# Gelu ahead of the probabilities, squares and sums a step sooner, a normalization behind the gate bank's reading

## The chip, the cores and the metric

The kernel runs on one core of a Trainium2 chip. What counts is the device time of one execution, in microseconds (us); a profile of one further execution shows when each engine worked. The engines are TensorE (PE, its weight loads PEld), VectorE (DVE), ScalarE (ACT), GpSimd (POOL) and SyncE (SP), which issues the transfers.

## What is computed

Two branches read the same 2048 tokens of 576 features, and a gate mixes them:

```
g = sigmoid((x * gate_w).sum(-1, keepdims=True))
a = attention with a memory(x, wq, wk, wv, wo, beta)      # 32 heads of 18, 4 segments of 512 tokens
    ...   p = softmax(q k^T * scale + mask); a_dot = p v  # inside a segment
b = (gelu(x @ w_gate) * (x @ w_up)) @ w_down              # 576 -> 4608 -> 576
out = g * a + (1 - g) * b
```

## The kernel before

Every float32 operand is split into two float16 words, high and low, and a product is made of three matmuls (high by high, high by low, low by high). After a first part of some 212 us (projections, memory), a loop of 72 steps `v` interleaves both branches; the change lies in its steps 3, 4 and 5, the fourth to sixth.

**The feed-forward branch in a step.** Step `v` takes 128 of the 4608 columns (`f = v // 2`) and two chunks of 512 tokens (`c` and `e`). Gate and up products of the two chunks are made together, in a form with seven products in place of eight; their sums grow in three PSUM banks, `V`, `G` and `U`. A step's PE work starts with the product `V` (`first_product`), then `G` from `A11`, which starts that bank anew. VectorE copies `V` to a tile `gl` (`g1`) and `G` to `U`; later `gl` plus a bank is the gate's value, ScalarE takes `gelu` of it in place, and `hidden` (L1073) multiplies it by what the bank `G` (chunk `c`) or `U` (chunk `e`) holds. Until that multiplication has read the bank, the next step's product cannot start in it. `hidden_pair` then makes the words `hh` on ScalarE and GpSimd. From step 4 on, `chains` (L1051) multiply an earlier block's `hh` by the down weights in the two banks `dn`, and VectorE adds them up (L1057).

**Attention in a step.** A unit `a` is one head in one segment; two units go through a step. `scores(a)` makes four products in banks `st` and `dn` (in the paired steps also `pv`); the pieces `put(a, i)` (L954) bring them to the tile `pf` with their row maxima. `powers` (L971, L974) takes the exponentials on ScalarE, `pair_rows` makes the words `ph` (ScalarE L984, GpSimd L985), `turn_rows` has SP issue their transposition (L991), `values` (L1005) multiplies by the values in bank `pv`, and `normalize` (L1015 to L1022) divides on VectorE. The odd unit of a head goes through `powers` and what follows in the next step.

**Weights for later steps.** `squares` sum the squares of raw weights (ScalarE L85 or VectorE L81), `sums()` turns them into scales: one small matmul into a bank `st` (L234), six short VectorE operations on it (L236 to L244) and six on GpSimd. `weights_first` scales or adds raw weights on GpSimd (L278, L299 to L303), `weights_high` and `weights_low` make their words (ScalarE L309, GpSimd L313).

The four compute engines issue in the order in which the code is written (`manual_schedule`), so where a call stands decides what waits behind it. SP's order is set by a scheduler. ScalarE holds one set of function tables: between exponentials and gelu it loads the other (`ACT_TABLE_LOAD`).

Steps 0 to 4 go through `step`, from step 5 on through `paired_step`; at the start of a step `end_pair` finishes what the former step left in `ends`.

Of the kernel before, what the change touches and what calls it, by code (L numbers as in the profile page):

```python
# [42 lines left out]
def kernel(ctx: ExitStack, tc: tile.TileContext, xs, wqk, wv, wo, wgu, wd, beta, out):  # L43
# [172 lines left out]
    def squares(fb, f, i, by=sum_squares):  # L216

        if f >= NF:
            return
        st = stat[fb % 2]  # L220
        if i < 2:
            r = raw_g[f][:, i * KT * P : (i + 1) * KT * P]
            o = st[:, 0, 2 * (f % 2) + i : 2 * (f % 2) + i + 1]
        else:
            r = raw_d[f]
            o = st[:, 1, f % 2 : f % 2 + 1]
        by(o, r)
# [662 lines left out]
    with tc.tile_pool(name="keep", bufs=2, side="right", reuse_waits="tile") as kp, ExitStack() as tail:  # L890
# [96 lines left out]
        def turn_rows(a):  # L987
            prob.pop(a)
            t, h = turned_p[a], pairs16.pop(a)
            for i in range(2):  # L990
                sp.dma_start(t[:, 10 * i : 10 * i + 10], h[:, i], transpose=True)  # L991
# [88 lines left out]
        def gelu(f, c, o, t):  # L1080
            act.activation(t, o, AF.Gelu_apprx_tanh, scale=scl[f // 2][0][:, 2 + c : 3 + c])  # L1081
# [22 lines left out]
        def weights_first(fb, i4):  # L1104
            n0 = 2 * fb
            if i4 == 0 and fb:
                scale_g(n0 + 1)
            if i4 == 1 and fb:
                sums_g(n0 + 1)
            if i4 == 2 and fb:  # L1110
                scale_g(n0 + 2)
                scale_d(n0)
            if i4 == 3 and fb:
                sums_g(n0 + 2)
                scale_d(n0 + 1)

        def weights_high(fb, i4):
            n0 = 2 * fb
            high_g(n0 + 1 + i4 // 2, i4 % 2)
            if i4 >= 2:  # L1120
                high_d(n0 + i4 - 2)
# [22 lines left out]
        def act_squares(v):  # L1144

            fb, i4 = divmod(v, 4)
            todo = {0: ((fb + 1, 2 * fb, 2),),
                    1: ((fb + 1, 2 * fb + 3, 0), (fb + 1, 2 * fb + 3, 1), (fb + 1, 2 * fb + 1, 2)),
                    2: ((fb + 2, 2 * fb + 4, 0), (fb + 2, 2 * fb + 4, 1))}
            todo = todo.get(i4, ()) if fb else ()  # L1150
            if v == 4:
                todo += (2, 4, 0), (2, 4, 1)
            for b, f, i in todo:
                squares(b, f, i, act_square)

# [10 lines left out]
        def end_pair(between=()):  # L1166

            for i, g in enumerate(ends):
                hidden(*g)
                if i == 0:  # L1170
                    for put in between:
                        put()
            for f, c, o, g in ends:
                hidden_pair(f, c, g)
            ends.clear()

        def paired_step(v):

            f, p = divmod(v, 2)
            fb, i4 = divmod(v, 4)  # L1180
            c, e = 2 * p, 2 * p + 1
            k = v - LAG
# [3 lines left out]
            def sums():  # L1186
                turns.update(of=0)
                scales(fb + 1)
                turns.update(of=2)
                scales_out(fb + 1)  # L1190

            put = puts.pop(2 * k - 1)
# [2 lines left out]
            x1, x2_, t = x16[c], x16[e], xt[p]  # L1195
            X, Y = bank("G"), bank("U")
            if ends:
                end_pair([lambda i=i: put(i) for i in (2, 3)])
            V, g1 = first_product(v), gl_tile()
            dve.tensor_copy(g1, V)  # L1200
            product(X, f, A11, x1, 0, 4, True)
# [3 lines left out]
            put(3)  # L1205
            late(0, 2)
            values(2 * k - 4)
            if v == LAG + 3:
                weights_first(fb, i4)
            if v == LAG + 3:  # L1210
                act_squares(v)
            for w in {0: ((fb + 1, 2 * fb, 2), (fb + 1, 2 * fb + 3, 0), (fb + 1, 2 * fb + 3, 1)),
                      2: ((fb + 2, 2 * fb + 4, 0),), 3: ((fb + 2, 2 * fb + 4, 1),)}.get(i4, ()):
                squares(*w, act_square)
            if i4 == 1 and v > LAG + 3:
                sums()
            weights_high(fb, i4)
            weights_low(fb, i4)
# [14 lines left out]
            values(2 * k - 3)  # L1233
            normalize(k - 2)
            late(6, 8)
            if v == LAG + 3:
                sums()
            if i4 == 3:
                load_v(fb + 1)
            product(Y, f, S1, t, 0, 2)  # L1240
# [45 lines left out]
        def step(v):  # L1286
# [4 lines left out]
            k = v - LAG  # L1291
# [44 lines left out]
            if v == 1:  # L1336
# [1 line left out]
                    high_d(n)  # L1338
                    low_d(n)
                scale_g(2)  # L1340
            if on(k - 1):
                powers(2 * k - 1)
                pair_rows(2 * k - 1, 0)
                pair_rows(2 * k - 1, 1)
                turn_rows(2 * k - 1)
            if v == 2:
                high_g(2, 0)
                low_g(2, 0)
                sums_g(2)
            if fb:  # L1350
                weights_high(fb, i4)
                weights_low(fb, i4)
            weights_load(fb, i4)
# [30 lines left out]
            if not fb and v != 3:  # L1384
                rest(X, f, U4, x1)
            some(fb - 1, early[2:3])
            for w in {2: (B22,), 4: (T1,)}.get(v - LAST, ()):
                low_w(w)
            product(Y, f, S1, t, 0, 2)
# [9 lines left out]
            if v != 3:  # L1399
                dve.tensor_tensor(g1, Y, g1, OP.add)  # L1400
            gelu(f, e, g1, g1)
            if v == 2:
                high_g(2, 1)
                low_g(2, 1)
            if fb:
                dve.tensor_tensor(g0, V, g0, OP.add)
                gelu(f, c, g0, g0)
            if fb or v == 3:
                product(X, f, A12, x1, 2, 6, part=range(3, 6))
                rest(X, f, U4, x1, (0,) if fb else (0, 1))  # L1410
# [29 lines left out]
            if fb and i4 == 1:  # L1440
                scales(fb + 1)
                scales_out(fb + 1)
            if v == 4:
                normalize(0)
            product(Y, f, S4, x2_, 2, 6, part=range(3, 6))
            rest(Y, f, UG, x2_, (0,) if fb else (0, 1))
            if fb:
# [226 lines left out]
```

## Time and profile before

| | |
|---|---|
| median of 3 runs | 1567.19 us (1566.99 to 1567.56) |
| the profiled execution | 1567.57 us, of them 1565.8 us span of instructions |
| PE busy | 1559.9 us |
| DVE, ACT, POOL busy | 1169.4, 1167.0, 1223.4 us |

The span is what the profile covers, from the first instruction to the last; the rest of the time lies around it. A matmul is shown until its result is out, and the next one starts before that, so PE can be shown busy while it waits a little.

### The profile page before, as it was taken

The page shows a single profiled execution, that of the slowest core. Times are in us where ns is not written, and L with a number is a line of the kernel's source. Part 1 is how long each engine was busy: PE and PEld are TensorE (multiplying, and loading weights), DVE is VectorE, ACT ScalarE, POOL GpSimd, SP SyncE. Part 2 cuts the span into 40 slices and gives each one's busy share as a digit, 9 for nine tenths or more (in the row PEclk, how much of TensorE's full clock was granted, in tenths as well). Part 3 has the DMA queues.
Part 4 walks back from the last instruction along what each step waited for, and adds up shares of the span by engine and source line. Part 5 has one row for each costly group of instructions (what it writes and reads, how often), then busy time and mean ns, then how long its engine had stood idle before and what let it go on. Part 6 is the DMA issues. An engine that isn't in the chain of part 4 may idle for free.

```text
span 1565.8 us, 32663 instructions
## 1 busy us (share of the span) xinstructions
PE 1559.9 (100%) x11902; PEld 940.7 (60%) x11902; DVE 1169.4 (75%) x2995; ACT 1167.0 (75%) x1973; POOL 1223.4 (78%) x1164
## 2 busy tenths in 40 slices
PE   9999999999999999999999999999999999999999
PEld 6665754556556555656555655655565655555577
DVE  6678876777778777777777777877777777776766
ACT  6666647888888788888888888878888888874310
POOL 3344867888888979898888888897989888887774
PEclk9999999999999999999999999999999999999999
DMA  6632445687878697778778777869788878746163
GB/s 219 226 124 103 148 142 95 118 155 122 140 124 144 122 150 137 130 133 133 141 128 134 138 139 126 150 128 145 142 130 138 133 133 137 137 71 138 42 144 99
DMA packets 472305, 209.00 MB, mean 133 GB/s; under 512 B 427600, under 2 KB 437072, under 8 KB 471632
## 3 DMA queue, kind: packets, MB, share of 16 engines
q1 hardware_dynamic: 472144, 206.92, 68.2%
q8 instruction: 93, 1.52, 0.4%
q14 instruction: 68, 0.56, 0.1%
HBM read 90.99 MB, written 27.26 MB: 76 GB/s over the span
## 4 chain that ended last, share of the span: by engine, by line
PE 94%; ACT 3%; DVE 1%; POOL 1%; issue 1%; DMA 0%; SPq 0%; ACTq 0%; DVEq 0%; POOLq 0%
PE dn L1051 26%; PE U L1091 17%; PE G L1091 12%; PE V L1091 11%; PE pv L1005 4%; PE U L1097 3%; PE st L333 2%; PE G L333 2%; PE dn L342 2%; PE V L1102 1%; PE U L333 1%; PE U L1554 1%; PE dn L948 1%; PE V L1097 1%; PE G L1097 1%; PE V L1554 1%
## 5 line engine op out<-in xcount | busy, mean ns | idle before, releaser
L1091 PEld LDWEIGHTS <-pairg 128*128 128x128 f16 x3024 | 285.7, 98 | 311.5 <-issue 18.5
L1051 PE MATMUL dn<-paird,hh 128*128 128x288 f16 x3408 | 466.0, 286 | 0.1
L1051 PEld LDWEIGHTS <-hh 128*128 128x128 f16 x3456 | 333.2, 98 | 124.7 <-issue 0.8
L985 POOL TENSOR_TENSOR ph<-pf,ph 128x512 f16<-128x512 f32 (+1 forms) x256 | 354.4, 1408 | 42.3 <-ACT ph L984 37.2
L1059 DVE SCALAR_TENSOR_TENSOR acc<-dn,ev,acc 128x288 f32<-128x288 f32 x536 | 264.4, 513 | 135.0 <-PE dn L1051 134.5
L974 ACT ACTIVATE pf<-pf,mb,esc 128x512 f32<-128x512 f32 (+3 forms) x512 | 293.0, 642 | 3.1
L1078 POOL TENSOR_TENSOR hh<-gl,hh 128x512 f16<-128x512 f32 x144 | 167.5, 1165 | 118.2 <-ACT hh L1077 118.2
L1091 PE MATMUL G<-x,pairg 128*128 128x512 f16 x864 | 212.0, 380 | 0.5 <-DVE gl L1073 0.4
L1091 PE MATMUL U<-xt,pairg 128*128 128x512 f16 x864 | 210.0, 379 | 0.0
L313 POOL TENSOR_TENSOR pairg<-raw,pairg 128x640 f16<-128x640 f32 (+2 forms) x144 | 174.9, 1238 | 18.9 <-ACT pairg L309 18.8
L1081 ACT ACTIVATE gl<-gl,sc 128x512 f32<-128x512 f32 x144 | 96.5, 714 | 104.2 <-DVE gl L1255 73.3
L984 ACT ACTIVATE ph<-pf 128x512 f16<-128x512 f32 (+1 forms) x256 | 172.4, 720 | 0.0
L1077 ACT ACTIVATE hh<-gl 128x512 f16<-128x512 f32 x144 | 89.5, 622 | 84.6 <-DVE gl L1073 84.5
L278 POOL TENSOR_SCALAR raw<-raw,sc 128x640 f32<-128x640 f32 x72 | 135.7, 1897 | 0.0
L1091 PE MATMUL U<-x,pairg 128*128 128x512 f16 x432 | 107.3, 379 | 0.0
L1091 PE MATMUL V<-xt,pairg 128*128 128x512 f16 x432 | 105.1, 379 | 0.0
L1091 PE MATMUL V<-x,pairg 128*128 128x512 f16 x432 | 104.8, 378 | 0.0
L309 ACT ACTIVATE pairg<-raw 128x640 f16<-128x640 f32 (+2 forms) x144 | 85.8, 641 | 20.1 <-POOL raw L303 14.1
L954 DVE CUSTOM_DVE_ANT_0 pf<-dn,mask 128x256 f32<-128x256 f32 (+1 forms) x195 | 95.7, 493 | 4.1 <-PE dn L948 4.1
L954 DVE CUSTOM_DVE_ANT_0 pf<-st,mask 128x512 f32<-128x512 f32 (+2 forms) x195 | 94.9, 510 | 0.0
L1073 DVE SCALAR_TENSOR_TENSOR gl<-G,sc,gl 128x512 f32<-128x512 f32 x72 | 54.0, 751 | 54.5 <-PE G L1097 32.0
L1005 PEld LDWEIGHTS <-pt 128*128 128x128 f16 x2560 | 83.1, 96 | 6.2
(317 smaller groups left out, 2713.9 us busy)
## 6 DMA issues: line engine op xcount, KB each, us to landing
raw<-in_wgu_dram SPq DMA_DIRECT2D x36, 640.0 KB
rawd<-in_wd_dram SPq DMA_DIRECT2D x36, 288.0 KB
qk<-stage SPq DMA_DIRECT2D x36, 256.0 KB
qt<-qk SPq DMA_DIRECT2D x128, 72.0 KB
kt<-qk SPq DMA_DIRECT2D x128, 72.0 KB
vp<-vstage SPq DMA_DIRECT2D x16, 296.0 KB
vt<-vp SPq DMA_DIRECT2D x16, 296.0 KB
qt<-qk SPq DMA_DIRECT2D x128, 36.0 KB
```

The lines of the kernel that those rows point to most:

```text
L278: pool.tensor_scalar(r, r, scl[f // 2][0][:, 0:1], None, OP.mult)
L313: pool.tensor_tensor(spot(f, *p, 1), raw_g[f][:, p[0] : p[1]], spot(f, *p, 0), OP.subtract)
L954: dve.tensor_tensor_reduce(prob[a][:, COL[qi] : COL[qi + 1]], outs.pop(i), mask[:, L - (qi + 1) * P :], 1.0, -3e38, OP.add, OP.max, mx[a][ ...
L974: act.activation(r, r, AF.Exp, bias=b[:, qi : qi + 1], scale=esc[:, 0, c : c + 1])
L984: act.activation(h[:, 0, cols], p[:, cols], AF.Copy)
L985: pool.tensor_tensor(h[:, 1, cols], p[:, cols], h[:, 0, cols], OP.subtract)
L1005: pe.matmul(ov, pr[:, 10 * i + COL[qi] // P + kb], v[:, 4 * e + kb, c0 : c0 + VC], start=kb == 0 and i == 0, stop=kb == qi and i == 1)
L1051: pe.matmul(o[:, :NH], hh[:, a, q * P : (q + 1) * P], w[:, b, n * NH : (n + 1) * NH], start=i == 0, stop=i == 5)
L1059: dve.scalar_tensor_tensor(av, o[:, :NH], ev, av, OP.mult, OP.add)
L1078: pool.tensor_tensor(hh[:, 1], t, hh[:, 0], OP.subtract)
L1081: act.activation(t, o, AF.Gelu_apprx_tanh, scale=scl[f // 2][0][:, 2 + c : 3 + c])
L1091: pe.matmul(o, w[:, i, (a + k) * P : (a + k + 1) * P], x[:, b + k], start=start and n == 0, stop=n == 5, skip_group_check=True)
```

## The change

ScalarE takes step 3's two gelus ahead of the exponentials of unit 1, and step 4's two ahead of the exponentials of unit 4 as before but without the squares and the weight words in front. Three squares of step 4 go from ScalarE to VectorE. What step 5 did for the weights at its start (three squares, the adding of raw weights) is done at the end of step 4, and its `sums()` stand before, not behind, its down chains 2 to 7. `normalize(0)` leaves the end of step 4 and stands in step 5 behind the `hidden` that reads bank `G`.

```diff
@@ act_squares
             if v == 4:
-                todo += (2, 4, 0), (2, 4, 1)
+                todo = ()
@@ paired_step
             if ends:
-                end_pair([lambda i=i: put(i) for i in (2, 3)])
+                end_pair([lambda: normalize(0)] * (v == 5) + [lambda i=i: put(i) for i in (2, 3)])
...
-            if v == LAG + 3:
-                weights_first(fb, i4)
-            if v == LAG + 3:
-                act_squares(v)
...
-            if i4 == 1 and v > LAG + 3:
+            if i4 == 1:
                 sums()
...
-            if v == LAG + 3:
-                sums()
@@ step
-            if on(k - 1):
+            def odd_rows():
                 powers(2 * k - 1)
                 pair_rows(2 * k - 1, 0)
                 pair_rows(2 * k - 1, 1)
                 turn_rows(2 * k - 1)
+
+            if on(k - 1) and v != 3:
+                odd_rows()
+            if v == 4:
+                squares(2, 4, 0)
+                squares(2, 4, 1)
...
-            if fb:
+            if fb and v > 4:
                 weights_high(fb, i4)
                 weights_low(fb, i4)
...
             some(fb - 1, early[2:3])
+            if v == 4:
+                squares(2, 2, 2)
...
             gelu(f, e, g1, g1)
+            if v == 3:
+                odd_rows()
...
+            if v == 4:
+                weights_high(fb, i4)
+                weights_low(fb, i4)
+                weights_first(fb, 1)
+                for w in ((2, 3, 2), (2, 5, 0), (2, 5, 1)):
+                    squares(*w, act_square)
...
-            if v == 4:
-                normalize(0)
```

What the scheduler's order shows, at three places. On ScalarE in step 3, before: unit 1's bias and exponentials (`mb`, `pf`), its high words (`ph`), then the tables of gelu and both gelus (`gl`), then the words `hh` of chunk `c`.

```order
L971 ACTIVATE mb<-mx,esc 128x4
L974 ACTIVATE pf<-pf,mb,esc 128x512
L974 ACTIVATE pf<-pf,mb,esc 128x128
L974 ACTIVATE pf<-pf,mb,esc 128x384
L974 ACTIVATE pf<-pf,mb,esc 128x256
L984 ACTIVATE ph<-pf 128x512
L984 ACTIVATE ph<-pf 128x768
L1081 ACT_TABLE_LOAD
L1081 ACTIVATE gl<-gl,sc 128x512 x2
L1077 ACTIVATE hh_2969<-gl 128x512
```

The same place of the changed kernel:

```order
L1081 ACT_TABLE_LOAD
L1081 ACTIVATE gl<-gl,sc 128x512 x2
L971 ACTIVATE mb<-mx,esc 128x4
L974 ACT_TABLE_LOAD
L974 ACTIVATE pf<-pf,mb,esc 128x512
L974 ACTIVATE pf<-pf,mb,esc 128x128
L974 ACTIVATE pf<-pf,mb,esc 128x384
L974 ACTIVATE pf<-pf,mb,esc 128x256
L984 ACTIVATE ph<-pf 128x512
L984 ACTIVATE ph<-pf 128x768
L1077 ACTIVATE hh_2969<-gl 128x512
```

The gelus went ahead of seven instructions, and the load of the exponentials' tables that stood behind them, in front of the next unit, came along. On VectorE at the start of step 5, where step 4 ends and `end_pair` runs, before:

```order
L1015 TENSOR_REDUCE pv<-pv 128x144
L1016 RECIPROCAL ord<-pv 128x8
L1019 SCALAR_TENSOR_TENSOR pv<-pv,gha,ord 128x72 x2
L1022 TENSOR_TENSOR ob<-ob,pv 128x8x18
L1073 SCALAR_TENSOR_TENSOR gl<-G,sc,gl 128x512
L954 ISA pf,mx<-dn,mask 128x256
```

And in the changed kernel:

```order
L1073 SCALAR_TENSOR_TENSOR gl<-G,sc,gl 128x512
L1015 TENSOR_REDUCE pv<-pv 128x144
L1016 RECIPROCAL ord<-pv 128x8
L1019 SCALAR_TENSOR_TENSOR pv<-pv,gha,ord 128x72 x2
L1022 TENSOR_TENSOR ob<-ob,pv 128x8x18
L954 ISA pf,mx<-dn,mask 128x256
```

The reading of bank `G` now comes first; the pieces of unit 3 in banks `dn`, and all of step 5 behind them, still have the normalization in front. On PE in step 5, the small matmul of `sums()`, which now stands behind the first product of the values and before the second product into bank `V`:

```order
 L1005 LDWEIGHTS pt
 L1005 MATMUL pv<-vt,pt 128x37
+L234 MATMUL st<-stat_88,ones 128x10
 L1091 LDWEIGHTS pairg
 L1091 MATMUL V<-x_1676,pairg 128x512
```

It left its place behind the last down chains of that step. PE's other instructions stand where they stood.

## Rows read from the trace of the kernel before

**Rows 1.** The page: busy time, share and instructions of each engine.

```profile
PE 1559.9 (100%) x11902; PEld 940.7 (60%) x11902; DVE 1169.4 (75%) x2995; ACT 1167.0 (75%) x1973; POOL 1223.4 (78%) x1164
```

**Rows 2.** Windows from one step's first `V` to the next: length, busy us by engine.

```profile
257.80:276.70 18.90, 18.46 (x150) 10.44 (x147) 12.46 (x34) 18.39 (x33) 14.18 (x11) 1.00 0.88 147
276.70:295.85 19.15, 18.81 (x152) 10.85 (x150) 14.11 (x39) 14.56 (x27) 14.20 (x14) 1.00 0.66 122
295.85:314.57 18.72, 18.59 (x148) 10.74 (x146) 14.63 (x40) 16.20 (x28) 18.04 (x19) 1.00 0.52 106
314.57:332.71 18.14, 18.14 (x148) 10.79 (x146) 13.27 (x37) 15.06 (x25) 16.75 (x17) 1.00 0.84 163
...
350.82:369.15 18.33, 18.33 (x149) 10.98 (x148) 14.87 (x45) 14.63 (x25) 14.93 (x19) 1.00 0.82 128
```

**Rows 3.** Timeline of PE: start, us, engine, line, operation, count, [idle before].

```profile
255.22 0.59 PE L1097 MATMUL G<-x,pairg 128*128 128x512 f16 x2
...
257.85 1.47 PE L1091 MATMUL V<-xt,pairg 128*128 128x512 f16 x6
259.75 1.46 PE L1091 MATMUL G<-x,pairg 128*128 128x512 f16 x6 [0.43 <-DVE gl L1073]
...
261.78 0.66 PE L1005 MATMUL pv<-vt,pt 128*128 128x37 f16 x20
...
271.75 0.66 PE L1005 MATMUL pv<-vt,pt 128*128 128x37 f16 x20
...
278.21 1.46 PE L1091 MATMUL G<-x,pairg 128*128 128x512 f16 x6
...
291.59 0.38 PE L1102 MATMUL G<-x,pairg 64*128 64x512 f16 x1
292.28 0.39 PE L948 MATMUL st<-kt,qt 54*128 54x384 f16 x2 [0.31 <-DVE pb L244]
...
297.31 1.46 PE L1091 MATMUL G<-x,pairg 128*128 128x512 f16 x6
...
311.00 0.38 PE L1102 MATMUL G<-x,pairg 64*128 64x512 f16 x1
311.01 0.38 PE L948 MATMUL st<-kt,qt 54*128 54x384 f16 x2
...
315.86 1.46 PE L1091 MATMUL G<-x,pairg 128*128 128x512 f16 x6
```

**Rows 4.** Timeline of ACT, steps 3 to 5.

```profile
252.50 0.62 ACT L1077 ACTIVATE hh<-gl 128x512 f16<-128x512 f32 x1
...
256.90 1.28 ACT L1081 ACT_TABLE_LOAD   x1
...
274.55 1.33 ACT L1081 ACTIVATE gl<-gl,sc 128x512 f32<-128x512 f32 x2
...
288.80 1.26 ACT L309 ACTIVATE pairg<-raw 128x640 f16<-128x640 f32 x2 [4.45 <-POOL raw L303]
...
295.14 1.33 ACT L1081 ACTIVATE gl<-gl,sc 128x512 f32<-128x512 f32 x2
```

**Rows 5.** Timeline of DVE around the starts of steps 4, 5 and 6.

```profile
258.95 0.75 DVE L1073 SCALAR_TENSOR_TENSOR gl<-G,sc,gl 128x512 f32<-128x512 f32 x1 [2.33 <-ACT gl L1081]
...
275.78 0.46 DVE L1015 TENSOR_REDUCE pv<-pv 128x144 f32<-128x288 f32 x1
...
277.41 0.74 DVE L1073 SCALAR_TENSOR_TENSOR gl<-G,sc,gl 128x512 f32<-128x512 f32 x1
...
296.50 0.75 DVE L1073 SCALAR_TENSOR_TENSOR gl<-G,sc,gl 128x512 f32<-128x512 f32 x1 [2.75 <-ACT gl L1081]
```

**Rows 6.** VectorE's squares at line L81, from 195 to 206 us: ns min/median/max.

```profile
L81 DVE CUSTOM_DVE_ANT_0 junk<-raw x2: 1594/1746/1899, 200.8 to 202.4; 128x640 bf16<-128x640 f32 x2
```

**Rows 7.** Timeline of POOL: low words of unit 0, first addition of raw weights.

```profile
251.94 2.76 POOL L985 TENSOR_TENSOR ph<-pf,ph 128x512 f16<-128x512 f32 x2 [1.71 <-ACT ph L984]
...
285.22 0.72 POOL L299 TENSOR_TENSOR raw<-raw 128x256 f32<-128x256 f32 x1
```

## The prediction

> **What bounds the kernel now.** I read the page's busy times first. PE is shown busy for 1559.9 of 1565.8 us [rows 1], the others for 75 to 78%. So the time is PE's own work, and a change that leaves PE's instructions alone, as this one does but for one small matmul that moves, can win only the places where PE waits. A matmul is shown until its result is out, so short waits hide inside busy time. I therefore looked at the starts, in the table of windows from one step's first product `V` to the next. From step 7 on a step takes 18.14 us, and 18.33 where `sums()` falls into it (every fourth) [rows 2]. Steps 4, 5 and 6 take 18.90, 19.15 and 18.72 [rows 2]. Step 5 carries a `sums()`, so it should take 18.33 and loses 0.82; step 6 should take 18.14 and loses 0.58. Step 4 has a make-up of its own, so I found its loss by the distance of two starts.
>
> PE's timeline shows where [rows 3]. Undisturbed, `G` starts 315.86 - 314.57 = 1.29 us behind its step's `V` [rows 2, 3].
> - Step 4: 259.75 - 257.85 = 1.90 us, so 0.61 lost. The view names VectorE's reading of `G` (L1073), and VectorE had itself stood idle for 2.33 us waiting for ScalarE's gelu [rows 5].
> - Step 5: 278.21 - 276.70 = 1.51, so 0.22 lost. Here VectorE had no wait: `normalize(0)` began at 275.78 and the reading of `G` stood behind it, at 277.41 [rows 5].
> - Step 5, late: a score product into `st` comes 0.69 us behind the `G` product that it normally accompanies at 0.01 [rows 3], so 0.68 lost; the releaser is the last short operation of `sums()` (L244), which still read that bank. The two of step 5 make 0.90, the windows 0.82; I use the windows.
> - Step 6: 297.31 - 295.85 = 1.46, 0.17 lost at `G`, and 0.41 later in the step. VectorE had waited 2.75 us for gelu before it could read `G` [rows 5]; all that it did afterwards was late. Gelu was late because ScalarE had waited 4.45 us for GpSimd's additions [rows 4].
>
> All that this change can reach is 0.61 + 0.82 + 0.58 = 2.01 us, 0.13% of the time.
>
> **The change part by part.**
>
> *Gelu first in step 3.* The last row of ScalarE before the moved block is `hh` at 252.50, 0.62 long; a table load takes 1.28 [rows 4], half of a pair of gelus 0.67 (1.33 for two [rows 4]). So the gelu of chunk `c` is done at about 255.1. Bank `G` is complete at 255.22 + 0.59 = 255.81 [rows 3], and VectorE, then idle, reads it until about 256.6. PE wants the bank at 257.85 + 1.29 = 259.14: 2.5 us to spare. The 0.61 goes. As many table loads as before are left, since the one of the exponentials moves along. What pays is unit 1: its exponentials and words come some 4 us later. ScalarE has one load less between units 1 and 2, so unit 2 starts about where it did. Unit 1's low words leave GpSimd at about 262.9 (my estimate: ScalarE's high words end near 260.9, GpSimd's two pieces take 2.76 [rows 7], less the overlap), and their transposition must land before PE's second `values`, at 271.75 - 0.61 = 271.14 [rows 3]: 8.2 us. Unit 0 had 261.78 - (251.94 + 2.76) = 7.08 us for the same way, with no wait on PE [rows 3, 7]. SP now issues four more transfers ahead of it, so this is cover with about a microsecond in hand, not certainty. Cost taken: 0.
>
> *Squares on VectorE in step 4.* Two squares of 640 columns are queued in front of the copy of `U` to `gl`, the third behind. ScalarE loses them, so its gelus of step 4, at 274.55 before [rows 4], start some 3 us sooner; nothing waited for them there but, at the end, the reading of `G`. On VectorE the squares start at about 262.4, when the last piece of unit 3 is out. The nearest rows are two of the same form: 1.59 and 1.90 us [rows 6], both while GpSimd worked (its own rows there are not shown). Lower bound 2 x 1.59 = 3.2, upper 2 x (1.90 + 0.08 for reading the sum) = 4.0. In step 4 GpSimd is at work too, with the words `hh` and `ph`. At the lower bound VectorE is free at 265.6, the copy (0.69) out at 266.3; by my reading of PE's order the product behind that copy is due at about 266.6. At the upper bound it waits 0.5. At the mean of the two rows, 1.75, it waits 0.1. I take 0, near that mean, and keep 0.5. The third square can hold the pieces of unit 4 by a further 0.15 at most.
>
> One rule speaks against this edit. The Trainium skill, page "SBUF — State Buffer", section "Who interferes with whom", states that a VectorE instruction with two SBUF inputs contends with a GpSimd instruction that reads SBUF, and that the second to issue blocks until the first is finished. The trace agrees as far as it goes: 1.59 and 1.90 us. By that rule a square waits for a whole GpSimd piece, which is the upper bound above: 0.5 to 0.65 us of the gain.
>
> *`normalize(0)` behind the reading of `G`.* It took 277.41 - 275.78 = 1.63 us of VectorE [rows 5]. With everything 0.61 sooner, `G` is complete before PE's next `V` starts at 276.09, is read by about 276.8, and PE wants it at 276.09 + 1.29 = 277.38. The 0.22 goes. But the 1.63 us is now in front of the two pieces in banks `dn`, of the reading of `U`, of the copy of `V` and of the first piece in `st`. Late next are, by my count, the first down chain (due 278.7, its bank free at 278.7 to 278.9) and the small matmul of `sums()` (due about 280.7, its bank free at 280.8 to 281.0), behind which PE's second product into `V` is queued. Bounds: 0, and the whole 1.63 if nothing covers it. I take 0.3, since in a regular step the same VectorE work starts well before it is due.
>
> *`sums()` sooner, squares and additions in step 4.* The small matmul costs PE what it costs in every such step, which 18.33 already holds. Its six VectorE operations are then over some 6 us before the score product needs the bank: the 0.68 goes. GpSimd's additions, which began at 285.22 [rows 7], run right behind the weight words of step 4, so the weight words of step 5 no longer hold ScalarE for 4.45 us [rows 4]. Step 5's gelus, begun at 295.14 [rows 4], can come 4.45 us sooner, more than the 2.75 by which VectorE waited [rows 5]. Then step 6 runs like step 7: 0.58 goes. The raw weights squared here were loaded long before, as ScalarE took them without a wait.
>
> **Sum.** 2.01 - 0.3 = 1.7 us. The profiled execution took 1567.57 us, 1.77 of them outside the span, and lies 0.38 above the median of 1567.19; the sum against it gives 1565.9, against the median, which a new measurement will be compared with, 1565.5. That is 0.11% less, below the 0.2% (3.1 us) that a measurement of this kernel tells from no change. The terms' bounds are 2.0 at best and, with 0.65 and 0.4 of waits, 1.0 at worst: 1565.2 to 1566.2, and some 0.3 either side for the spread of the runs.
>
> **Rivals.**
> - *The squares wait for GpSimd* (chance 0.14). Both at 1.9 us and more, as in the slower of the two rows [rows 6]: 0.65 off the gain, 1566.2 us. For it: GpSimd's words of unit 1 and of chunk `c`, some 4 and 2 us later than before, now fall into that stretch. Against: at the mean of the two rows it costs 0.1.
> - *VectorE becomes the bound of step 5* (0.07). The 1.63 us of the normalization come out on PE in full, since chains, `sums()` and copies hang on one queue: 2.01 - 1.63 = 0.4 us, 1566.8. It decides from the point at which the reading of `G` starts later than about 276.5.
> - *No change* (0.05). Something else, a transfer perhaps, stands close behind each of the removed waits: 1567.2.
> - *Slower: unit 1's transposed words come too late* (0.04). From 271.14 on each microsecond of lateness is one of PE's. Slower than before by anything needs them 2 us late, slower by over 0.2% 5 us, at 276.2: 13 us after GpSimd, where unit 0 shows that 7.08 are enough [rows 3, 7]. Then 1570.3 us.
> - *Faster by over 0.2%* (0.02): there is not so much waiting in this stretch, so it would need a wait that the trace hides.
>
> **How the numbers follow.** The forecast, 1565.5 us, has 0.68. Its own range of 1564.8 to 1566.5 and the first rival make 0.82; with a margin for my estimated starts the range is 1564.8 to 1566.9. Every case but the last two is within 0.2%: same 0.94, slower 0.04, faster 0.02.
>
> **What would show it.** In the profile after: `G` 1.29 us behind `V` in steps 4, 5 and 6; the first `V` of step 5 at 276.1, of step 6 at 294.7, of step 7 at 312.8 to 313.0 instead of 314.57; no wait of a product into `st` for L244; ScalarE's gelu of step 3 done by 255.8. Step 5 between 18.4 and 18.7 us says how much the normalization costs. The prediction is wrong if PE waits at the second `values` of step 4 for a transfer, at the product behind the copy of `U` in step 4, or at the small matmul of `sums()` for more than half a microsecond.

## The result and the profile after

| | before | after |
|---|---|---|
| median of 20 runs, us | 1567.38 (1566.99 to 1568.85) | 1569.92 (1568.72 to 1570.88) |
| profiled execution / its span, us | 1567.57 / 1565.8 | 1569.69 / 1568.0 |
| step 4, first `V` to first `V` | 18.85 | 22.52 |
| step 5 | 19.15 | 18.61 |
| step 6 | 18.72 | 18.11 |

The kernel became 2.54 us slower: ratio 1.0015 [1.0009, 1.0021], which does not reach the 0.2% named in the prediction, but is outside its range and on the other side of no change. The steps account for all of it: +3.67 - 0.54 - 0.61 = +2.52 us. (The window of step 4 in [rows 2] begins 0.05 us ahead of the first `V`, hence 18.85 here and 18.90 there. The two profiled executions differ by 2.12 us only, as step 4's first `V` comes 0.40 us sooner in the second; that lead is there before step 3 begins.) Steps 5 and 6 came out near the forecast, though rows_alone below shows that a long step 4 shortens them by itself. Step 4 was to lose 0.61 us and gained 3.67.

The page of after, its line of busy times:

```profile
PE 1560.5 (100%) x11902; PEld 941.8 (60%) x11902; DVE 1173.7 (75%) x3001; ACT 1165.0 (74%) x1967; POOL 1225.3 (78%) x1164
```

Its windows from one step's first `V` to the next, with columns as in [rows 2]; the second row is a stretch inside step 4, and the column behind the engines is the granted clock:

```profile
257.45:279.97 22.52, 19.71 (x149) 10.99 (x147) 14.94 (x37) 18.68 (x35) 19.53 (x14) 0.92 0.89 142
262.64:266.05 3.41, 3.02 (x29) 1.91 (x29) 3.41 (x12) 2.76 (x6) 2.88 (x3) 0.50 1.14 78
279.97:298.58 18.61, 18.56 (x152) 11.04 (x149) 16.37 (x45) 13.25 (x22) 13.65 (x18) 1.00 0.66 129
```

As in [rows 1], the page's busy shares say nothing: 0.6 us more on PE. The windows say which step, and the clock's column says that step 4 holds something that no row of before has: 0.92, because PE was granted half its clock, 1.2 GHz, from 262.64 to 266.05.

The timeline of after from step 3's gelu to step 4's squares:

```profile
254.04 1.34 ACT L1081 ACTIVATE gl<-gl,sc 128x512 f32<-128x512 f32 x2
...
256.14 0.75 DVE L1073 SCALAR_TENSOR_TENSOR gl<-G,sc,gl 128x512 f32<-128x512 f32 x1
...
256.88 2.29 ACT L974 ACTIVATE pf<-pf,mb,esc 128x512 f32<-128x512 f32 x4
...
257.45 1.47 PE L1091 MATMUL V<-xt,pairg 128*128 128x512 f16 x6
258.76 1.46 PE L1091 MATMUL G<-x,pairg 128*128 128x512 f16 x6
259.07 1.35 ACT L984 ACTIVATE ph<-pf 128x512 f16<-128x512 f32 x2
259.76 2.75 POOL L985 TENSOR_TENSOR ph<-pf,ph 128x512 f16<-128x512 f32 x2 [4.05 <-ACT ph L984]
...
262.54 0.42 DVE L954 CUSTOM_DVE_ANT_0 pf<-dn,mask 128x256 f32<-128x256 f32 x1 [4.54 <-POOL ph L985]
...
263.03 1.59 PE L1051 MATMUL dn<-paird,hh 128*128 128x288 f16 x6 [2.81 <-DVE mx L954]
...
264.15 2.76 POOL L985 TENSOR_TENSOR ph<-pf,ph 128x512 f16<-128x512 f32 x2 [0.53 <-POOL hh L1078]
...
265.81 1.79 DVE L81 CUSTOM_DVE_ANT_0 junk<-raw 128x640 bf16<-128x640 f32 x1
...
266.84 0.38 PE L1097 MATMUL V<-x,pairg 128*128 128x512 f16 x1
266.87 1.75 POOL L1078 TENSOR_TENSOR hh<-gl,hh 128x512 f16<-128x512 f32 x1
...
267.64 1.66 DVE L81 CUSTOM_DVE_ANT_0 junk<-raw 128x640 bf16<-128x640 f32 x1
```

Read from the top. The gelu of chunk `c`, the first of the two, is done at about 254.7 (forecast 255.1, in a profile that runs 0.40 us later; in [rows 4] its table load came only at 256.90), `G` is read at 256.14 with no wait for it, and PE's `G` stands 258.76 - 257.45 = 1.31 us behind `V`, where [rows 3] have 1.90: the first gain is there. Then the price. Unit 1's exponentials (L974) stand behind that gelu, so its high words (L984) and GpSimd's low words (L985) are late, until 262.51. At 262.54 VectorE begins unit 3's pieces (L954), after standing idle for 4.54 us, and the wait names L985: the pieces go into a tile `pf`, there are two of these, and the one that unit 3 gets is unit 1's, whose last reader is GpSimd. Until the pieces are taken out of bank `dn`, PE's first down chain cannot write there. It was due 1.29 us behind `G`, at 260.05, and began at 263.03: 2.98 lost. The half clock then costs PE 1.29 more: from this down chain to the first matmul of L1097 it takes 266.84 - 263.03 = 3.81, where rows_alone below, at full clock, takes 2.52. 18.85 - 0.61 + 2.98 + 1.29 = 22.51, against 22.52.

The timeline of after in step 5:

```profile
279.97 1.47 PE L1091 MATMUL V<-xt,pairg 128*128 128x512 f16 x6
...
281.28 1.46 PE L1091 MATMUL G<-x,pairg 128*128 128x512 f16 x6
...
288.31 0.15 DVE L244 TENSOR_SCALAR pb<-st 128x4 int32<-128x4 int32 x1
...
295.02 0.38 PE L948 MATMUL st<-kt,qt 54*128 54x384 f16 x2
...
295.51 1.38 ACT L1081 ACTIVATE gl<-gl,sc 128x512 f32<-128x512 f32 x2 [4.23 <-DVE gl L1249]
```

`G` is 1.31 behind `V` in step 5 too; L244 is done 6.6 us before the scores into `st`; ScalarE's gelu waits for its input and no longer for GpSimd's additions ([rows 4] have 4.45 there). In the view of waits, VectorE's for L985 (4.5 us) and PE's for L954 (2.8) are new; those of `G` for L1073 in these steps and of `st` for L244 are gone.

### The profile page after: what moved, and what is told of

Read it like the earlier page. It is cut to its first block, busy times and chain, and to the rows that moved or that the text cites. A ratio compares the mean times of both kernels' runs of the same rounds, so it can differ in the third digit from the quotient of the medians.

```text
span 1568.0 us, 32667 instructions
## 1 busy us (share of the span) xinstructions
PE 1560.5 (100%) x11902; PEld 941.8 (60%) x11902; DVE 1173.7 (75%) x3001; ACT 1165.0 (74%) x1967; POOL 1225.3 (78%) x1164
## 4 chain that ended last, share of the span: by engine, by line
PE 97%; DVE 1%; ACT 1%; POOL 0%; issue 0%; POOLq 0%; DVEq 0%
PE dn L1051 27%; PE U L1091 18%; PE G L1091 12%; PE V L1091 12%; PE pv L1005 4%; PE U L1097 3%; PE st L333 2%; PE G L333 2%; PE dn L342 2%; PE V L1102 1%; PE U L333 1%; PE U L1562 1%; PE dn L948 1%; PE V L1097 1%; PE G L1097 1%; PE G L1102 1%
## 5 line engine op out<-in xcount | busy, mean ns | idle before, releaser
L1051 PE MATMUL dn<-paird,hh 128*128 128x288 f16 x3408 | 466.5, 286 | 2.8 <-DVE mx L954 2.8
L1051 PEld LDWEIGHTS <-hh 128*128 128x128 f16 x3456 | 333.4, 98 | 127.6 <-issue 3.5
L985 POOL TENSOR_TENSOR ph<-pf,ph 128x512 f16<-128x512 f32 (+1 forms) x256 | 354.5, 1408 | 40.9 <-ACT ph L984 35.3
L974 ACT ACTIVATE pf<-pf,mb,esc 128x512 f32<-128x512 f32 (+3 forms) x512 | 293.0, 642 | 3.1
L1078 POOL TENSOR_TENSOR hh<-gl,hh 128x512 f16<-128x512 f32 x144 | 168.1, 1170 | 120.8 <-ACT hh L1077 120.8
L984 ACT ACTIVATE ph<-pf 128x512 f16<-128x512 f32 (+1 forms) x256 | 172.4, 720 | 2.0 <-DMA pt<-ph 2.0
L954 DVE CUSTOM_DVE_ANT_0 pf<-dn,mask 128x256 f32<-128x256 f32 (+1 forms) x195 | 95.7, 493 | 7.9 <-POOL ph L985 4.5
L954 DVE CUSTOM_DVE_ANT_0 pf<-st,mask 128x512 f32<-128x512 f32 (+2 forms) x195 | 95.0, 511 | 0.0
L1073 DVE SCALAR_TENSOR_TENSOR gl<-G,sc,gl 128x512 f32<-128x512 f32 x72 | 54.0, 751 | 50.8 <-PE G L1097 32.7
```

What stands on the lines that cost most here:

```text
L954: dve.tensor_tensor_reduce(prob[a][:, COL[qi] : COL[qi + 1]], outs.pop(i), mask[:, L - (qi + 1) * P :], 1.0, -3e38, OP.add, OP.max, mx[a][ ...
L974: act.activation(r, r, AF.Exp, bias=b[:, qi : qi + 1], scale=esc[:, 0, c : c + 1])
L984: act.activation(h[:, 0, cols], p[:, cols], AF.Copy)
L985: pool.tensor_tensor(h[:, 1, cols], p[:, cols], h[:, 0, cols], OP.subtract)
L1051: pe.matmul(o[:, :NH], hh[:, a, q * P : (q + 1) * P], w[:, b, n * NH : (n + 1) * NH], start=i == 0, stop=i == 5)
L1078: pool.tensor_tensor(hh[:, 1], t, hh[:, 0], OP.subtract)
```

## The experiments

The theory after this result: what costs is that unit 1's words come late and keep `pf`, and the half clock is a consequence of PE's idle time there. The first rival: the squares on VectorE, which stand in the same step. Step lengths are distances of the first `V`s in one profiled execution of each kernel; medians are of 6 to 11 runs, the ratios against medians of 1566.84 to 1567.05 of the kernel before, measured beside them. The steps tell more than the medians: step 3's first `V` stands between 242.6 and 243.8 us in these profiles, ahead of every edit, and what follows step 7 takes 1233.1 to 1233.2 us in all. A third buffer for `pf`, the plain test, was not tried, so the part of `pf` is shown by the order of the work and by the wait's name alone.

| kernel | step 4 | 5 | 6 | median us | ratio [95%] |
|---|---|---|---|---|---|
| rows_back | 18.86 | 18.75 | 18.11 | 1566.23 | 0.9995 [0.9986, 1.0004] |
| rows_alone | 21.23 | 18.46 | 18.11 | 1570.72 | 1.0021 [1.0011, 1.0030] |
| filled_wait | 22.00 | 18.61 | 18.11 | 1569.11 | 1.0013 [1.0004, 1.0022] |
| chain_later | 18.29 | 19.20 | 18.11 | 1566.14 | 0.9993 [0.9984, 1.0002] |
| sums_behind | 18.33 | 19.15 | 18.11 | 1566.07 | 0.9993 [0.9984, 1.0003] |
| norm_early | 18.26 | 18.77 | 18.11 | 1565.88 | 0.9993 [0.9984, 1.0003] |
| sums_late | 19.00 | 20.88 | 18.11 | 1567.15 | 1.0002 [0.9993, 1.0012] |
| squares_vector | 23.68 | 19.33 | 18.12 | 1571.69 | 1.0030 [1.0018, 1.0042] |
| front_behind | 18.30 | 19.37 | 18.11 | 1565.79 | 0.9993 [0.9983, 1.0003] |
| front_early | 18.26 | 18.66 | 18.11 | 1565.62 | 0.9993 [0.9983, 1.0002] |
| words_behind | 18.37 | 18.86 | 18.11 | 1566.14 | 0.9994 [0.9984, 1.0003] |
| words_early | 18.26 | 19.02 | 18.11 | 1565.69 | 0.9993 [0.9983, 1.0002] |

**rows_back and rows_alone: the rest of the change without the move of unit 1's words, and that move without the rest.** In rows_back the changed kernel gets the old order of step 3; in rows_alone the kernel before gets the new one and nothing else. The edit of rows_back:

```diff
-            if on(k - 1) and v != 3:
+            if on(k - 1):
                 odd_rows()
...
-            if v == 3:
-                odd_rows()
```

> The changed kernel with unit 1's exponentials, words and transposition back in front of step 3's gelus; all else of the change stays, the squares on VectorE too. Theory (the tile pf has two buffers, so the pieces of unit 3 wait until GpSimd has read unit 1's, and that reading was moved 3.9 us later): step 4 falls from 22.52 us to about the 18.85 of the kernel before, no wait of a dn chain for L954, no fall of the clock; steps 5 and 6 keep 18.6 and 18.1. About 1566.2 us, 1.1 below the kernel before. Rival (the squares on VectorE, or the normalization, made step 4 long): step 4 stays near 22.5 us and the time near 1569.9.

> The kernel before with this one move alone: unit 1's exponentials, words and transposition behind step 3's gelus. Theory (buffer of pf): the first dn chain of step 4 waits about 3 us, the clock falls to half for some 3 us behind it, step 4 takes about 22.5 us; steps 5 and 6 stay at about 19.1 and 18.7. About 1571.0 us. Rival (squares on VectorE): step 4 takes about 18.2 us, 1566.8 us.

The timeline of rows_back, step 4:

```profile
255.89 2.75 POOL L985 TENSOR_TENSOR ph<-pf,ph 128x512 f16<-128x512 f32 x2
...
259.42 1.46 PE L1091 MATMUL G<-x,pairg 128*128 128x512 f16 x6 [0.44 <-DVE gl L1073]
...
260.71 0.90 PE L1051 MATMUL dn<-paird,hh 128*128 128x288 f16 x6
...
263.19 0.82 DVE L81 CUSTOM_DVE_ANT_0 junk<-raw 128x640 bf16<-128x640 f32 x1
```

The timeline of rows_alone, step 4, and one row of step 5 that is needed further down:

```profile
263.02 0.90 PE L1051 MATMUL dn<-paird,hh 128*128 128x288 f16 x6 [2.81 <-DVE mx L954]
...
265.54 0.38 PE L1097 MATMUL V<-x,pairg 128*128 128x512 f16 x1
...
292.71 0.16 DVE L241 TENSOR_SCALAR v<-z 128x2 int32<-128x2 int32 x1
```

With the old order the low words are out at 258.64, the down chain follows `G` by 1.29 and the old wait at `G` is back: 18.86 against 18.85 expected, although the squares are still on VectorE. With the new order alone the wait of 2.81 us is there to the hundredth, with no square on VectorE. The squares are ruled out as the cause of this wait, the move is shown. Step 4 of rows_alone is 18.85 - 0.61 + 2.98 = 21.22, measured 21.23: this profiled execution stayed at full clock, which I had not expected. Nor had I expected its steps 5 and 6 to shorten to 18.46 and 18.11 with nothing changed there. While PE loses 3 us in step 4, the other engines go on, and what they were late with afterwards is ready. So the gains of steps 5 and 6 in the changed kernel, whose step 4 is long too, can't be put down to its edits; those of rows_back can, 18.75 and 18.11 behind a step 4 of 18.86.

The clock falls in some executions and not in others. The runs of rows_alone go from 1568.27 us (this profiled one) to 1571.78: three have a mean clock of 1.000 (up to 1569.41), seven of 0.999 (from 1569.24). Of the changed kernel's twenty runs six have 1.000. The spread of rows_alone, 3.5 us, is more than the 1.29 of one fall; what the rest is, no kept trace shows.

**filled_wait: thirteen matmuls of 512 columns in PE's wait.** They write bank `U`, which is overwritten later, so what is computed stays as it was. The timeline shows PE busy where it stood idle.

```diff
+            if v == 4:
+                for n in range(13):
+                    pe.matmul(Y, pair_g[f][:, 0, A11 * P : (A11 + 1) * P], x1[:, 0], start=True, stop=True,
+                              skip_group_check=True)
```

> The changed kernel with 13 matmuls of 512 columns more, whose sums nobody reads, put into bank U behind step 4's product G, where PE waits for the piece of unit 3. Theory (2.98 us of the loss are the wait itself, 1.28 us the half clock that follows PE's idle time): the wait is filled with 2.8 us of matmuls, the granted clock stays at its upper level, step 4 takes about 21.2 us and the time is about 1568.6, less than with the wait empty. Rival (the fall of the clock does not come from that idle time): it falls again, step 4 stays at 22.5 us or more, 1569.9 us.

```profile
259.92 2.97 PE L1311 MATMUL U<-x,pairg 128*128 128x512 f16 x13
262.90 0.90 PE L1051 MATMUL dn<-paird,hh 128*128 128x288 f16 x6
...
265.69 1.77 DVE L81 CUSTOM_DVE_ANT_0 junk<-raw 128x640 bf16<-128x640 f32 x1
...
267.50 1.66 DVE L81 CUSTOM_DVE_ANT_0 junk<-raw 128x640 bf16<-128x640 f32 x1
...
269.82 1.46 PE L1091 MATMUL U<-xt,pairg 128*128 128x512 f16 x6 [0.60 <-DVE gl L1371]
```

The mean clock is 1.000 in all ten runs, which lie within 0.5 us (1568.85 to 1569.37) where the changed kernel's span 2.2. So PE's idle time is what the clock fell for. The step is 22.00 and not 21.23 as in rows_alone: the copy of `U` stands behind two squares of 1.77 and 1.66 us, and PE waits for it, 0.60 by the row and 0.77 by the step. In the changed kernel's profile the slow clock hides this wait: while PE loses 1.29 us, VectorE gets on with its squares. Hence the step gains 0.52 and not 1.29.

**chain_later: the new order of step 3, with the work that waits for it put behind other work.** In step 4 the copies of `V` and `G` go ahead of unit 3's pieces, the first down chain behind the product into `U`, and the squares back to ScalarE.

```diff
-                    end_pair([lambda i=i: put(2 * k - 1, i) for i in (2, 3)])
+                    end_pair([lambda i=i: put(2 * k - 1, i) for i in (2, 3)] if v != 4 else ())
...
+            if v == 4:
+                for i in (2, 3, 0):
+                    put(3, i)
...
-            if v == 4:
-                squares(2, 4, 0)
-                squares(2, 4, 1)
```

> The changed kernel with three squares of step 4 back on ScalarE, and in step 4 VectorE's copies of V and of G ahead of unit 3's pieces, and the first down chain behind the product into U, together with the second. Theory (buffer of pf): the pieces still wait until GpSimd is done at about 262.5 us, but PE has the values, the second product into V and that into U to do until about 263.3, so it waits 0.3 us at most and the clock stays up; step 4 takes about 18.3 to 18.6 us, steps 5 and 6 18.6 and 18.1, 1565.5 to 1566.0 us. Rival (something else in step 4 holds PE, such as unit 0's or unit 1's transposed words): a wait of a pv product for a transfer, step 4 over 19.5 us.

The timeline of chain_later, in step 4:

```profile
262.70 0.42 DVE L954 CUSTOM_DVE_ANT_0 pf<-dn,mask 128x256 f32<-128x256 f32 x1 [1.59 <-POOL ph L985]
...
263.55 1.63 PE L1051 MATMUL dn<-paird,hh 128*128 128x288 f16 x12
```

And in step 5:

```profile
282.50 2.76 POOL L985 TENSOR_TENSOR ph<-pf,ph 128x512 f16<-128x512 f32 x2 [1.20 <-ACT ph L984]
...
282.77 0.91 DVE L241 TENSOR_SCALAR v<-z 128x2 int32<-128x2 int32 x1
...
283.72 1.57 DVE L243 TENSOR_SCALAR v<-v 128x2 int32<-128x2 int32 x1
...
285.83 1.63 PE L1051 MATMUL dn<-paird,hh 128*128 128x288 f16 x12 [0.43 <-DVE acc L1057]
```

The pieces still wait for the low words, 1.59 us by their row, but PE has other work: step 4 is 18.29, the 0.61 won and nothing lost. So the mechanism is settled. Step 5, though, is 19.20 where the same code takes 18.61 in the changed kernel: VectorE's small integer operations of `sums()`, L241 and L243, take 0.91 and 1.57 us beside GpSimd's words, and the additions behind them are late. The next runs take this apart, and try the prediction's other terms one by one.

**sums_behind, norm_early, sums_late, squares_vector.** All start from chain_later. In sums_behind `sums()` of step 5 stands behind the second pair of chains; in the others, one edit of the change is undone or restored on top of that.

```diff
-            if i4 == 1:
+            if i4 == 1 and v > 5:
                 sums()
...
             late(2, 4)
+            if v == 5:
+                sums()
```

> The kernel of the run chain_later with one more edit: in step 5 the sums of squares and their scales (L234 to L258) are issued behind the second pair of down chains and VectorE's additions of them (L1057), not ahead. Theory, that VectorE's integer operations (L241 0.91, L243 1.57 us beside GpSimd's low words) held up the additions for which the next chains waited: steps 4, 5, 6 = 18.3, 18.6, 18.1, and 0.6 us less than chain_later, about 1565.6. Rival, that step 5 is late there for what step 4 left undone: step 5 stays at 19.2, 1566.2.

> As sums_behind, with the first normalization back at its old place at the end of step 4, so the one term of the sum that this edit is alone. By the prediction's step: the gate bank's reading stands behind 1.6 us of VectorE again, the product into G starts 0.22 us later (V to G 1.53 instead of 1.31) and step 5 is 18.8; if the normalization's own 0.3 us, charged to step 5, then goes away, 18.5. Rival, that the reading waits for the matmuls into G and not for VectorE's queue: step 5 stays at 18.6.

> As sums_behind, with the sums of squares at the late place that they had before the change, behind the chains 6 and 7 of step 5. By the prediction's step: the scores into st wait 0.68 us for the last of VectorE's integer operations (L244), step 5 is 19.3, about 1566.3. Rival, that this wait was there only because the normalization and the late squares held VectorE up: step 5 stays at 18.6, 1565.6.

> As sums_behind, with the three squares of step 4 on VectorE, where the change put them, so the squares' own price in a step without the 2.98 us wait. The prediction's term: 0, step 4 stays at 18.3, 1565.6. Theory after filled_wait, where the copy of U was late behind them: VectorE takes 1.6 to 1.8 us for each of the first two beside GpSimd, the copy of U comes late and TensorE waits 0.4 to 0.9 us, step 4 is 18.7 to 19.2, 1566.0 to 1566.5.

norm_early adds `if v == 4: normalize(0)` at its old place and takes it out of `end_pair`; sums_late has the call of `sums()` further down, behind chains 6 and 7, where it was before the change; squares_vector has the calls of `squares(2, 4, 0)`, `squares(2, 4, 1)` and `squares(2, 2, 2)` where the change put them.

The timeline of sums_behind, step 5:

```profile
282.00 1.63 PE L1051 MATMUL dn<-paird,hh 128*128 128x288 f16 x12
282.51 2.76 POOL L985 TENSOR_TENSOR ph<-pf,ph 128x512 f16<-128x512 f32 x2 [1.19 <-ACT ph L984]
...
284.43 0.87 DVE L241 TENSOR_SCALAR v<-z 128x2 int32<-128x2 int32 x1
...
286.42 0.69 DVE L1229 COPY gl<-U 128x512 f32<-128x512 f32 x1
...
287.59 1.63 PE L1051 MATMUL dn<-paird,hh 128*128 128x288 f16 x12 [0.56 <-DVE acc L1057]
```

The forecast failed, the theory did not. The wait of 0.43 went and one of 0.56 came at the next chain, for `sums()` now stands in front of the copy of `U` (286.42) and the additions behind that. And its two integer operations are long again: L241 took 0.87 us and ended at 285.30, as GpSimd's words did (282.51 + 2.76 = 285.27); L243, 1.08 long, ended at 286.41, as a half of GpSimd's L1078 did (286.39). At the time I took this for GpSimd holding the copy itself, and the last four runs were made for that.

The timeline of norm_early, step 5:

```profile
274.94 1.47 PE L1091 MATMUL V<-xt,pairg 128*128 128x512 f16 x6
...
276.45 1.46 PE L1091 MATMUL G<-x,pairg 128*128 128x512 f16 x6
...
281.22 1.63 PE L1051 MATMUL dn<-paird,hh 128*128 128x288 f16 x12
...
283.65 0.47 DVE L241 TENSOR_SCALAR v<-z 128x2 int32<-128x2 int32 x1
...
286.41 1.63 PE L1051 MATMUL dn<-paird,hh 128*128 128x288 f16 x12 [0.16 <-DVE acc L1057]
```

`G` is 276.45 - 274.94 = 1.51 behind `V`, 0.20 more than in sums_behind, as the term of 0.22 says; but by the second down chain the two are level, 281.22 - 274.94 = 6.28 behind `V` against 282.00 - 275.74 = 6.26 in sums_behind. So the place of the normalization wins 0.20 and costs about as much by then. That step 5 is 0.38 shorter here, with a wait of 0.16 in place of 0.56, comes later, from L241: 0.47 us in place of 0.87.

The timeline of sums_late, step 5:

```profile
294.02 0.39 PE L948 MATMUL st<-kt,qt 54*128 54x384 f16 x2 [0.99 <-DVE pb L244]
```

The scores into `st` wait 0.99 us for L244, more than the 0.68 expected. There is more: step 5 took 20.88, a down chain waited 0.92 us for VectorE, and step 4 was 19.00, 0.46 of it a wait for a transposition. Only the first wait belongs to the edit for certain, and L243 took 1.56 us ahead of it, where it took 1.08 before. This profile is of the slowest of the ten runs, 1.56 us above their median, so the others need not look like it.

The timeline of squares_vector, step 4:

```profile
264.29 1.79 DVE L81 CUSTOM_DVE_ANT_0 junk<-raw 128x640 bf16<-128x640 f32 x1
...
266.12 2.14 DVE L81 CUSTOM_DVE_ANT_0 junk<-raw 128x640 bf16<-128x640 f32 x1
...
269.35 0.90 PE L1051 MATMUL dn<-paird,hh 128*128 128x288 f16 x6 [3.62 <-DVE acc L1057]
```

Far beyond what I gave it. The squares take 1.79 and 2.14 us beside GpSimd, the additions behind them free bank `dn` late, PE stands for 3.62 us, and the clock falls to half from 270.25 to 273.66, as it did in the changed kernel:

```profile
270.25:273.66 3.41, 3.41 (x11) 1.04 (x11) 1.19 (x3) 2.61 (x3) 3.41 (x3) 0.50 0.91 105
```

That the additions for this chain stand behind the squares is owed to chain_later's order; in filled_wait PE waited for the copy of `U` alone.

**front_behind, front_early, words_behind, words_early: why GpSimd is late in step 5.** The three squares that the change put on ScalarE at the end of step 4 turn out to run ahead of the exponentials of step 4's last unit. They were put behind those exponentials (front) or behind the words (words), on sums_behind and on norm_early. The edit of words_behind and words_early:

```diff
                 pair_rows(2 * k, 0)
                 pair_rows(2 * k, 1)
                 turn_rows(2 * k)
+            if v == 4:
+                for w in ((2, 3, 2), (2, 5, 0), (2, 5, 1)):
+                    squares(*w, act_square)
...
                 weights_first(fb, 1)
-                for w in ((2, 3, 2), (2, 5, 0), (2, 5, 1)):
-                    squares(*w, act_square)
```

> As sums_behind, with the three squares that the change put on ScalarE at the end of step 4 issued earlier, between the probabilities and their words (behind L974, ahead of L984). In sums_behind the wait of 0.56 us for VectorE's additions had only moved to the next chain, and the copy of U ahead of those additions began as GpSimd's first half of L1078 ended. Theory, that GpSimd is late there because ScalarE's exponentials of step 5 stand behind those three squares: they begin some 1 to 2 us earlier, the copy of U waits for TensorE again as in the changed kernel, steps 4, 5, 6 = 18.3 to 18.6, 18.6, 18.1, 0.5 us less than sums_behind. Rival, that VectorE itself is full in step 5 (1.6 us of normalization more): step 5 stays at 19.1.

> As norm_early, with the same move of the three squares on ScalarE ahead of the words. Theory: the 0.16 us wait for VectorE's additions goes, the 0.20 us at the gate bank stays, steps 4, 5, 6 = 18.3 to 18.6, 18.55 to 18.6, 18.1. Rival, that the squares in front of the words make the transposed words late: TensorE waits for pt in step 5 and it is 18.8 or more.

> As sums_behind, with the three squares that the change put on ScalarE at the end of step 4 issued behind the words of those probabilities (behind L984 of the rows that step 4 ends with), so that nothing but the exponentials is ahead of the words and GpSimd can begin its low words (L985) some 2.4 us earlier; in front_behind the squares stood between them and GpSimd began no earlier. Theory, that GpSimd's late halves of L1078 hold the copy of U, VectorE's additions and so the chains: the 0.56 us wait goes, steps 4, 5, 6 = 18.3, 18.6, 18.1, 0.5 us less than sums_behind. Rival, that VectorE itself is full in step 5: step 5 stays at 19.1.

> As norm_early, with the same move of the three squares behind the words. Theory: the 0.16 us wait for VectorE's additions goes, the 0.20 us at the gate bank stays, steps 4, 5, 6 = 18.3, 18.55 to 18.6, 18.1, about 1565.5. Rival, that the sums of squares then wait for ScalarE's late squares (L234): step 5 is 18.8 or more.

front_behind did not test what I meant: the squares stood between exponentials and words, GpSimd's low words began no earlier (6.99 us behind `V`, 6.77 in sums_behind), and step 5 grew to 19.37. words_behind did, as its timeline shows:

```profile
284.05 2.27 POOL L1078 TENSOR_TENSOR hh<-gl,hh 128x512 f16<-128x512 f32 x2
...
284.60 0.62 DVE L241 TENSOR_SCALAR v<-z 128x2 int32<-128x2 int32 x1
...
287.48 1.63 PE L1051 MATMUL dn<-paird,hh 128*128 128x288 f16 x12 [0.28 <-DVE acc L1057]
```

L985 starts 5.4 us behind `V`, L1078's first half ends at 285.2, and L241, 0.62 us long, ends with it. The wait halves, to 0.28, and step 5 is 18.86. On top of norm_early it went the other way, 19.02 against 18.77; front_early gave 18.66.

How step 5 depends on where GpSimd's pieces fall shows when L241 is put beside the step in the six kernels that have `sums()` at this place and ScalarE's squares:

| | sums_behind | norm_early | front_behind | front_early | words_behind | words_early |
|---|---|---|---|---|---|---|
| L241, us | 0.87 | 0.47 | 1.10 | 0.35 | 0.62 | 0.75 |
| step 5, us | 19.15 | 18.77 | 19.37 | 18.66 | 18.86 | 19.02 |
| difference | 18.28 | 18.30 | 18.27 | 18.31 | 18.24 | 18.27 |

Step 5 is 18.24 to 18.31 us plus the time of this one operation on two numbers a partition. In each of the six L241 ends 0.02 to 0.03 us after a piece of GpSimd's L985 or L1078, so what it takes is what is left of that piece when its turn comes; in rows_alone, with GpSimd idle, it takes 0.16. That L241 waits for the piece is read from these times and from no run of its own.

By their profiles chain_later, sums_behind, norm_early, front_early, words_behind and words_early take 1.1 to 1.7 us out of the three steps, front_early the most. Its median is 1.22 us below before's, but its interval holds 1, as does that of each of the six.

## Why the prediction was wrong

- **The failed step** is "Gelu first in step 3 ... Cost taken: 0". Its gain came: `G` is 1.31 behind `V`, and step 4 takes 18.86 with the old order and 18.29 with the new one once nothing is lost there. The estimate of unit 1's low words was right, too: 262.9, measured 262.51 in a profile that runs 0.40 us sooner. But I asked only who needs the *result* of those words, the transposition for PE's second `values`, and found a cover of a microsecond. I did not ask who needs the *tile* that they read. Unit 3's pieces do, being two units on in a pool of two, and they hold the bank of a down chain due at 260.05. In front of that wait there was no cover: 2.98 us, shown by rows_alone and taken away by chain_later. The slower rival, unit 1's words late for the transposition, had the right source and the wrong consumer: no `values` of step 4 waited for a transfer. It asked for words that miss 271.14 by 2 us before anything is lost; low words that end 262.51 - 258.64 = 3.9 us later than in rows_back were enough. None of the three waits that were named as signs of being wrong came in the changed kernel; the one that came was not among them.
- **A term missing altogether** is the clock. 2.4 us into PE's idle time of 2.81 us the clock fell to half, for 3.41 us in the profiled execution: 1.29 us more. No row of before had PE idle for more than 0.43 us in these steps, so its trace could not price it.
- **Squares on VectorE**, taken 0, at most 0.65: in the changed kernel the durations are as bounded, 1.79 and 1.66 against 1.59 to 1.90, and in filled_wait the waiter is the one named, the product behind the copy of `U`. In the profile of the changed kernel it costs nothing that shows, being hidden by the slow clock; with full clock it costs 0.60 to 0.77 (filled_wait). The term was mis-sized; it belonged at or above its upper bound, the first rival's. The bounds came from two rows beside GpSimd and do not hold in general: 0.82 in rows_back, where GpSimd was idle, 2.14 in squares_vector.
- **`normalize(0)`**: 0.22 won at `G` is right (1.31; 0.20 in norm_early). Step 5 came out at 18.61, forecast 18.33 + 0.3. That agreement is partly luck: step 4 was 3 us too long there and gave the other engines a lead. In rows_back, without that lead, step 5 is 18.75, so 0.42 above 18.33. By sums_behind and norm_early, one profile each, the place of the normalization is worth nothing either way: 0.20 won and about as much lost by the second down chain. What made step 5 long or short in the last six kernels is a term that the sum did not have, L241's wait for GpSimd's piece. The rival "VectorE becomes the bound of step 5" was worth more than its 0.07, and not for the normalization.
- **`sums()` sooner**: right, but the changed kernel alone does not show it. The wait for L244 is gone, in rows_back too, and comes back, at 0.99, when `sums()` goes back; gelu's 4.45 is gone. Step 6 is 18.11, forecast 18.14, in rows_back as in the changed kernel. In rows_alone step 6 is 18.11 as well, though the edit is not in it.

A kernel like chain_later keeps 1.1 us of the forecast 1.7 by its steps, 0.9 by its median (1566.14 against 1567.05), and that is not told from no change by its interval.

## What to carry to other kernels

When work is moved later, list for each of its instructions not only who reads what it writes, but who will overwrite what it reads: with a pool of two, the unit after the next waits for the last reader, on any engine. A wait that makes TensorE stand still for some microseconds can cost more than its length (here 2.98 us and 1.29 more), so price it against a row of the trace with idle time of that size, or say that there is none. And a wait that is taken away shows the next one behind it: a gain measured while another stall hides things is not that edit's gain.

## What the hardware showed unexpectedly

- **Clock.** TensorE idle from 260.22 to 263.03 (2.81 us, L1051 in after) was granted 0.50, 1.2 GHz, from 262.64 on, for 3.41 us. Idle for 3.62 us until 269.35 (squares_vector), it was granted 0.50 from 270.25 on, when it was at work again, for 3.41 us too. At the same wait of 2.81 us rows_alone's profiled execution kept full clock. With the wait filled by matmuls the mean clock was 1.000 in all ten runs.
- **VectorE and GpSimd hold each other up, both ways.** A square took 0.82 us with GpSimd idle (rows_back) and 1.66 to 2.14 beside it, and GpSimd's L1078 took 1.75 us in after where one half takes 1.14. They take turns there: GpSimd's words end at 264.15 + 2.76 = 266.91, the square that began at 265.81 ends 0.69 later, at 267.60, and L1078, begun at 266.87, 1.02 after that. The Trainium skill, page "SBUF — State Buffer", section "Who interferes with whom", says that the port pair shared by the two engines is an exclusive lock; the trace agrees, and shows that GpSimd pays as well as VectorE.
- **Small integer operations wait too.** L241 (two numbers a partition) took 0.16 us in rows_alone with GpSimd idle, 0.35 in front_early and 1.10 in front_behind, L243 0.16, 1.08 and, beside GpSimd's low words, 1.57 in chain_later; in step 5 of these kernels, rows_alone aside, each ended 0.02 to 0.03 us after a piece of GpSimd did.
